# Zero fills of a gradient kernel: 56 KB rows for the last fills of the software queue

## The chip, the cores and the metric

The kernel runs on one core of one Trainium2 chip. The time is the device time of that core, in microseconds, for one launch. TensorE multiplies, VectorE and ScalarE do the elementwise work and empty PSUM, and 16 DMA engines move data between the device memory and the on-chip memory. Transfers are issued by SyncE and ScalarE (two hardware queues, q1 and q10 in the profile) and by GpSimd, which the profile calls POOL (one software queue, q0). [...]

## The reference

One decoding step of a network and the gradients of all its inputs: a layer norm, an attention that reads only the last W = 4096 rows of a cache of 32768, a gate from a small network with a squared ReLU, and a residual sum.

```python
W = min(4096, max(256, Sk // 4))
k = jnp.repeat(k_cache[:, :, Sk - W:, :], rep, axis=1)
v = jnp.repeat(v_cache[:, :, Sk - W:, :], rep, axis=1)
scores = jnp.einsum("bhqd,bhkd->bhqk", q, k) * (Dh ** -0.5)
p = _softmax(scores, axis=-1)
o = jnp.einsum("bhqk,bhkd->bhqd", p, v)
...
s = _A_ref(xn, A_k_cache, A_v_cache, A_wq, A_wo)
g = _silu(_B_ref(xn, B_w1, B_b1, B_w2, B_b2))
return x + s * g
...
_out, _vjp = jax.vjp(_f, A_x, A_k_cache, A_v_cache, A_wq, A_wo, B_w1, B_b1, B_w2, B_b2)
```

The sizes are: batch 2, one query position, model width 512, 32 query heads and 8 cache heads of 128, hidden width 1792 in the gate. All data is bf16. The outputs are the result and nine gradients. The gradients of the K cache and of the V cache (out_2 and out_3) have the shape of the caches, 2 x 8 x 32768 x 128 each. Only the last 4096 rows of each head are not zero: the other 28672 rows of each of the 32 pairs of batch and head are zeros that the kernel has to write.

## The kernel before

**Zero fills.** There are 32 fills of 28672 rows of 256 bytes, 7168 KB each, one per pair of cache and head; `zparts` (line 105) lists them. 31 are issued by GpSimd in the loop at lines 115 to 120, ahead of everything else on that engine, so they run in their order 0 to 30 on the software queue. Their source is one tile of zeros, `zt`, of 128 partitions and 112 x 128 bytes, and the transfer converts its uint8 to the type of the destination. The function `zf` (line 90) makes one transfer. A "row" here is one descriptor: a contiguous stretch of the output.

Most fills write two times 128 rows of 112 cache rows each, as bf16, so a descriptor is 28 KB. The fills listed in `zlong` (line 107) write 128 rows of 224 cache rows: there `zf` views the destination as 32-bit, so that the same 14336 elements of `zt` fill 56 KB. Five fills listed in `zshort` are cut into several transfers of other sizes. A fill is issued when the one eight transfers before it has landed. The last fill, number 31, is issued by SyncE at line 623, directly after the store of the gradient of w1 (line 618), and it waits for fill 29 of the software queue (line 624).

**Start.** SyncE loads w1, w2, wo, wq and the first V tile; the small network, the projections and the transposes of the weights follow (lines 216 to 347).

**Four rounds** (line 422), one for each batch and group of four cache heads. A round takes a V tile and a K tile of 4 MB (`nat`, 128 partitions of 32 KB) and computes scores, softmax and the gradients. `outer_store` (line 404) writes the gradient of the V tile over the tile itself and stores it from ScalarE's queue (line 414), then SyncE loads the next V tile into the same memory; the same for K. In round 3, the last one, there is no next load.

**Epilogue** (from line 498). The memory of the cache tiles is freed and given to the tiles of the epilogue, of which `o_rows` (line 502) is the first. ScalarE issues the store of the gradient of wq (line 500). Then come a chain of small steps, the store of the gradient of w2 (line 610), that of w1 (line 618), the last fill (line 623) and that of wo (line 630).

Of the kernel before, what the change touches and what calls it, by code (L numbers as in the profile page):

```python
# [16 lines left out]
def kernel(  # L17
# [86 lines left out]
    ZQ = 2 * B * HKV  # L104
    zparts = [(out_2, q) for q in range(B * HKV)] + [(out_3, q) for q in range(B * HKV)]

    zlong = (3, 5, 7, 11, 12, 16, 17, 18, 19, 22, 23, 24, 28)
    zshort = {
        2: ((5, 8, 2), (120, 68, 3), (128, 32, 1), (16, 1, 1)),
        4: ((3, 1, 2), (2, 99, 6), (128, 112, 1), (128, 102, 1), (86, 1, 1)),  # L110
# [547 lines left out]
```

## Time and profile before

| | |
|---|---|
| median of 6 runs | 775.14 us |
| the six runs | 766.73, 767.09, 767.11, 783.18, 799.6, 800.37 us |
| the profiled execution | 766.91 us |
| its span, first to last instruction | 765.1 us |
| busy share of TensorE / VectorE / ScalarE / GpSimd | 54% / 36% / 28% / 4% |
| bytes moved | 326.73 MB, mean 427 GB/s |
| q0, the fills from GpSimd | 227.55 MB, 70.4% of the 16 engines' time |
| q1, SyncE's transfers | 56.63 MB, 18.8% |
| q10, ScalarE's transfers | 41.95 MB, 12.9% |

The profile is that of one execution. "Busy" counts an engine's instructions, and a matmul's end is modelled. In the slices, a digit is the busy share of a fortieth of the span in tenths. In answers on DMA, a line gives a queue's packets, MB and the share of 16 engines' time; shares of a short window can go a little over 100%, since a packet counts whole by its start. In the chain and in the order of time, a line begins with the start and the length in us. `L414` is line 414 of the kernel.

### The profile page before, as it was taken

The page shows a single profiled execution, that of the slowest core. Times are in us where ns is not written, and L with a number is a line of the kernel's source. Part 1 is how long each engine was busy: PE and PEld are TensorE (multiplying, and loading weights), DVE is VectorE, ACT ScalarE, POOL GpSimd, SP SyncE. Part 2 cuts the span into 40 slices and gives each one's busy share as a digit, 9 for nine tenths or more (in the row PEclk, how much of TensorE's full clock was granted, in tenths as well). Part 3 has the DMA queues.
Part 4 walks back from the last instruction along what each step waited for, and adds up shares of the span by engine and source line. Part 5 has one row for each costly group of instructions (what it writes and reads, how often), then busy time and mean ns, then how long its engine had stood idle before and what let it go on. Part 6 is the DMA issues. An engine that isn't in the chain of part 4 may idle for free.

```text
span 765.1 us, 9402 instructions
## 1 busy us (share of the span) xinstructions
PE 414.8 (54%) x4118; PEld 271.7 (36%) x4118; DVE 277.2 (36%) x484; ACT 214.8 (28%) x313; POOL 30.3 (4%) x56
## 2 busy tenths in 40 slices
PE   0166776548800774891086847502654886176770
PEld 0153365435300673450045734102543543134220
DVE  3033343238510343842033455401323755024760
ACT  0034341044510123661011145500114355100350
POOL 3000010010000000000000000000000000000000
PEclk9997889686765796786558968755968677575555
DMA  9999999999999999999999999999999999999998
GB/s 353 432 427 428 438 423 431 437 430 429 421 436 428 433 436 435 424 428 433 428 430 438 439 430 422 430 433 433 439 436 428 420 433 429 441 422 428 427 429 364
DMA packets 12473, 326.73 MB, mean 427 GB/s; under 512 B 2276, under 2 KB 2284, under 8 KB 2294
## 3 DMA queue, kind: packets, MB, share of 16 engines
q0 software_dynamic: 8000, 227.55, 70.4%
q1 hardware_dynamic: 2696, 56.63, 18.8%
q10 hardware_dynamic: 1736, 41.95, 12.9%
q8 instruction: 32, 0.52, 0.3%
q14 instruction: 9, 0.07, 0.0%
HBM read 45.62 MB, written 280.50 MB: 426 GB/s over the span
## 4 chain that ended last, share of the span: by engine, by line
DMA 38%; PE 32%; DVE 15%; ACT 8%; issue 4%; ACTq 0%; DVEq 0%; SPq 0%
DMA out_dram<-nat 16%; DMA nat<-in_A_k_cache_dram 14%; PE ov L410 6%; PE s_ps L383 4%; DMA b_bf<-in_B_b_dram 4%; DMA nat<-in_A_v_cache_dram 4%; PE tp L377 4%; DVE tT L156 3%; DVE ds_bf L457 2%; ACT p_bf L444 2%; DVE nat L156 2%; PE wps L628 2%; ACT nat L154 2%; PE dops L308 1%; PE ps L399 1%
## 5 line engine op out<-in xcount | busy, mean ns | idle before, releaser
L377 PE MATMUL tp<-pperm,nat 128*128 128x128 bf16 x1024 | 85.7, 235 | 142.8 <-DMA nat<-in_A_v_cache_dram 111.2
L156 DVE COPY tT<-tp 128x1024 bf16<-128x1024 bf16 x96 | 64.1, 689 | 212.6 <-PE tp L377 212.0
L377 PEld LDWEIGHTS <-nat 128*128 128x128 bf16 x1024 | 74.9, 107 | 149.6 <-DMA nat<-in_A_v_cache_dram 113.1
L154 ACT COPY tT<-tp 128x1024 bf16<-128x1024 bf16 x32 | 32.4, 1012 | 273.8 <-PE tp L377 273.8
L154 ACT CAST nat<-ov 128x512 bf16<-128x512 f32 x160 | 87.6, 589 | 53.2 <-PE ov L410 52.0
L156 DVE CAST nat<-ov 128x512 bf16<-128x512 f32 x96 | 65.4, 690 | 49.2 <-PE ov L410 48.0
L410 PE MATMUL ov<-bd,ds_bf 128*128 128x512 bf16 x128 | 48.1, 454 | 5.8 <-DVE nat L156 3.9
L410 PE MATMUL ov<-bd,p_bf 128*128 128x512 bf16 x128 | 48.9, 451 | 4.3 <-DVE nat L156 1.8
L101 POOL DMA_DIRECT2D out_dram<-zt x47 | 28.7, 615 | 533.8 <-DMA out_dram<-zt 530.6
L383 PE MATMUL dp_ps<-tT,zdo 128*128 128x256 bf16 x256 | 42.2, 298 | 14.2 <-DVE tT L156 8.2
L383 PE MATMUL s_ps<-tT,zq 128*128 128x256 bf16 x256 | 40.0, 282 | 14.5 <-DVE tT L156 9.4
L383 PEld LDWEIGHTS <-zdo 128*128 128x128 bf16 x256 | 25.9, 105 | 22.9 <-issue 19.3
L399 PE MATMUL ps<-t,nat 128*128 128x16 bf16 x1024 | 28.5, 173 | 7.8 <-DVE bd L367 7.8
L383 PEld LDWEIGHTS <-zq 128*128 128x128 bf16 x256 | 24.9, 101 | 21.5 <-issue 19.0
L399 PEld LDWEIGHTS <-nat 128*128 128x128 bf16 x1024 | 28.5, 103 | 11.0 <-issue 5.8
L495 PE MATMUL wps<-dq_rows,xn_bf 2*128 2x512 bf16 x32 | 13.4, 485 | 24.3 <-ACT wq L154 19.0
L391 PE MATMUL tp<-ident_bf,p_bf 128*128 128x128 bf16 x64 | 7.5, 312 | 34.9 <-ACT p_bf L444 34.9
L444 ACT ACTIVATE p_bf<-e_sb,rl 32x512 bf16<-32x512 f32 x16 | 22.8, 1423 | 3.4 <-DVE rl L441 3.3
L156 DVE CAST wq<-wps 128x512 bf16<-128x512 f32 x16 | 11.0, 690 | 31.5 <-PE wps L495 31.1
L154 ACT CAST dw_st<-wps 128x512 bf16<-128x512 f32 x15 | 8.8, 587 | 47.9 <-PE wps L608 45.1
L457 DVE SCALAR_TENSOR_TENSOR ds_bf<-dp_ps,delta,p_bf 32x512 bf16<-32x512 f32 x16 | 21.7, 1357 | 0.3
L410 PEld LDWEIGHTS <-ds_bf 128*128 128x128 bf16 x128 | 13.0, 108 | 22.9 <-issue 19.7
(197 smaller groups left out, 458.6 us busy)
## 6 DMA issues: line engine op xcount, KB each, us to landing
out_dram<-zt POOLq DMA_DIRECT2D x26, 7168.0 KB, 162.0
out_dram<-nat ACTq DMA_DIRECT2D x8, 4096.0 KB, 28.4
nat<-in_A_v_cache_dram SPq DMA_DIRECT2D x4, 4096.0 KB, 30.5
nat<-in_A_k_cache_dram SPq DMA_DIRECT2D x4, 4096.0 KB, 30.3
out_dram<-zt POOLq DMA_DIRECT2D x4, 3584.0 KB, 56.2
out_dram<-zt SPq DMA_DIRECT2D x1, 7168.0 KB, 36.0
out_dram<-zt POOLq DMA_DIRECT2D x1, 6120.0 KB, 86.2
wo<-in_A_wo_dram SPq DMA_DIRECT2D x1, 4096.0 KB, 37.5
```

Of the source, the lines that this page charges most:

```text
L101: sw_fill.append(nc.gpsimd.dma_start(out=v, in_=zs))
L154: nc.scalar.copy(out=out_ap, in_=in_ap)
L156: nc.vector.tensor_copy(out=out_ap, in_=in_ap)
L308: nc.tensor.matmul(dops[0:B, :, :], lhsT=dsT_bf[:, dk, :], rhs=woT[:, :, dk, :], start=(dk == 0), stop=(dk == DK - 1))
L377: nc.tensor.transpose(tp[:, j, :], nat[:, g * CC + half * CH + j, :], pperm[:].rearrange("p b k -> p (b k)"))
L383: nc.tensor.matmul(out_ps[:, half * CH * PB:(half + 1) * CH * PB], lhsT=zbuf[:, pr, o:o + R], rhs=tT[:, :, pr, :], start=(g == 0 and pr == ...
L399: nc.tensor.matmul(ps[:], lhsT=nat[:, g * CC + half * CH + cc, :], rhs=cols[half][:, cc, :, g, :], start=(half == 0 and g == 0 and cc == 0 ...
L410: nc.tensor.matmul(ov[:], lhsT=src[:, cc].rearrange("r k b -> r (k b)"), rhs=bd[:, gh * 4:(gh + 1) * 4, :], start=True, stop=True)
L444: nc.scalar.activation(out=p_bf[rb, :, :, pr], in_=e_sb[rb], func=ACT.Copy, scale=rl[rb, 0:1])
L457: nc.vector.scalar_tensor_tensor(out=ds_bf[rb, :, :, pr], in0=dp_c[rb], scalar=delta[rb, 0:1], in1=p_bf[rb, :, :, pr], op0=ALU.subtract, o ...
L495: nc.tensor.matmul(wps[:], lhsT=xn_bf[:, k:D:DK], rhs=dq_rows[:, :], start=True, stop=True)
L628: nc.tensor.matmul(wps[:], lhsT=o_rows[:, j:N:NJ], rhs=ds_rows[:, :], start=True, stop=True)
```

## The change

Four numbers, 26, 27, 29 and 30, are added to `zlong`. Fill 28 is there already, so the last five fills of the software queue are all written as 128 descriptors of 56 KB. Fill 25 keeps its descriptors of 28 KB, and fill 31 on SyncE's queue is not touched.

```diff
-    zlong = (3, 5, 7, 11, 12, 16, 17, 18, 19, 22, 23, 24, 28)
+    zlong = (3, 5, 7, 11, 12, 16, 17, 18, 19, 22, 23, 24, 28, 26, 27, 29, 30)
```

The order of the fills, their bytes and all other instructions stay as they are.

## The prediction

> **What bounds the kernel now.** I read the slices of the page first. Below them stands the rate that the 16 DMA engines moved in each fortieth of the span.
>
> ```profile
> DMA  9999999999999999999999999999999999999998
> GB/s 353 432 427 428 438 423 431 437 430 429 421 436 428 433 436 435 424 428 433 428 430 438 439 430 422 430 433 433 439 436 428 420 433 429 441 422 428 427 429 364
> ```
>
> Between the first slice and the last the engines never idle and the rate stays near 430 GB/s. The kernel is as long as its 326.73 MB take. An edit that moves the same bytes can gain only by a better rate, and loses whatever time it leaves the engines without work. So I asked two things: does a 56 KB row move faster than two of 28 KB, and can the engines run dry? The row kinds, from DMA answers for windows of 10 us in which only the software queue (q0) moves data: 600 to 610 (28 KB rows), then 670 to 680 (56 KB rows).
>
> ```profile
> q0 software_dynamic: 148, 4.24, 100.2%
> ```
>
> ```profile
> q0 software_dynamic: 76, 4.36, 102.5%
> ```
>
> Columns are packets, MB and the share of 16 engines. A 28 KB row takes 1.002 x 160 engine-us / 148 = 1.083 us, a 56 KB row 1.025 x 160 / 76 = 2.158 us, twice 1.079. Per byte they are the same.
>
> Next, what the rows do to others. The same view for 648 to 658, where the last store of round 3 (q10, 32 KB rows) runs beside 28 KB fills, and for 541 to 550, where a cache load (q1, 32 KB rows) runs beside 56 KB fills:
>
> ```profile
> q10 hardware_dynamic: 66, 2.16, 50.8%
> q0 software_dynamic: 73, 2.09, 49.0%
> ```
>
> ```profile
> q0 software_dynamic: 47, 2.52, 65.2%
> q1 hardware_dynamic: 45, 1.47, 39.2%
> ```
>
> The two queues take turns row by row, whatever the row is long: 66 to 73, and 47 to 45. A 32 KB row takes 0.508 x 160 / 66 = 1.23 us. So a store loses speed when the fills beside it have longer rows.
>
> Which transfer matters is in the waits of ScalarE, in the chain that ended last (start, length), and in the DMA issues of ScalarE and SyncE in order of time:
>
> ```profile
> ACT o_rows L154 <- DMA out_dram<-nat: 20.4, 1, 20.4
> ```
>
> ```profile
> 638.66 25.43 DMA out_dram<-nat
> ...
> 664.19 1.00 ACT o_rows L154
> ```
>
> ```profile
> 617.24 0.56 ACTq L414 DMA_DIRECT2D out_dram<-nat  x1
> 638.66 0.55 ACTq L414 DMA_DIRECT2D out_dram<-nat  x1
> 672.12 0.37 ACTq L500 DMA_DIRECT2D out_dram<-wq  x1
> 742.59 0.35 ACTq L630 DMA_DIRECT2D out_dram<-wo  x1
> ```
>
> ```profile
> 720.82 0.33 SPq L610 DMA_DIRECT2D out_dram<-dw_st  x1
> 727.80 0.33 SPq L618 DMA_DIRECT2D out_dram<-dw_st  x1
> 728.18 0.43 SPq L623 DMA_DIRECT2D out_dram<-zt  x1
> ```
>
> The epilogue's first tile, o_rows, lies in the memory of the cache tiles, so it waits for the K store of round 3, from 638.66 to 664.09. From there a chain of small steps leads to the dw1 store (727.80), the last fill behind it on SyncE (728.18) and the wo store (742.59). Meanwhile the software queue has work until about 730.8. The cover is thin: the late transfers are issued 3 us before it is used up.
>
> **What the Trainium skill says.** "DMA: Bandwidth & Descriptors", section "Queues, rings and completion order", says that each engine goes round the queues that have work at packet granularity, draining a packet before it switches, and that a packet typically holds 9 to 17 descriptors. The first half agrees (47 turns to 45); here a turn is one row of up to 56 KB. The same page, "Issuing engines are not separate DMA queues", says that transfers from all engines interleave on the same 16; the windows above show that. Its "Specifications" give a ceiling of 435 GB/s; the page's 420 to 441 between the first slice and the last say that longer rows have nothing to win.
>
> **The change part by part.** Fill 28 has 56 KB rows already, so four fills change: 26, 27, 29 and 30. Each issues 128 rows where it issued 256, the same 7.34 MB, in the same order. Counting 256 rows per short fill back from the switches in the row sizes (594, 664, 685), fill 26 is served from about 612, 27 until 664, 28 from there to 685, 29 and 30 until 731. Up to 612 nothing changes: POOL issues a fill when the fill eight before it has landed, and the last issue is at 563.48, before any changed row is served.
>
> *Rows saved*: 512 rows fewer, each pair at most 2 x 1.083 - 2.158 = 0.008 us cheaper. 512 x 0.008 / 16 = 0.26 us, within the reading error. I take zero (bounds 0 and -0.3). Fewer rows to generate costs POOL nothing: it idles 126.7 us before its next instruction.
>
> *V store, issued 617.24*. Its issue does not move, since no load is outstanding after 557. Its first rows appear at 623.7: queue 10 moves nothing from 617.3 to 623.5. That is 6.5 us, the time of rows already queued ahead. The wq store shows the same with 56 KB rows ahead: issued 672.12, no row before 682.5, its first ones by 682.7, so 10.6 us. The V store then starts at 617.24 + 10.6 = 627.8. It has 128 rows, 8 for each engine, and each waits for a turn of the fills: 8 x (1.23 + 2.16) = 27.1 us, done at 654.9. Before it was 8 x (1.23 + 1.08) = 18.5, and 623.7 to 641.8 was measured.
>
> *K store, issued 638.66*. It now queues behind the V store and follows with no gap: another 27.1 us, done at 682.0. Before, its last row ended at 662.7 and the landing was seen at 664.1, so I add 1.4: 683.4. The delay is X = 683.4 - 664.1 = 19.3 us. Bounds: if the V store still starts at 623.7 and each takes 26 us (what a load from 531.5 to 557.5 took, mostly beside 56 KB rows), X = 623.7 + 52 + 1.4 - 664.1 = 13. If the fills get 148 rows to 128 (the count over that load), a store takes (128 x 1.23 + 148 x 2.16) / 16 = 29.8 and X = 627.8 + 59.6 + 1.4 - 664.1 = 24.7. I take the even turns.
>
> *What queues behind*. ScalarE stops at o_rows; behind it are its copies of wq, so TensorE waits too (19.0 us now), then the whole chain from 664 on. I move it as a block by X: wq store at 691.4, dw2 store 740.1, dw1 store 747.1, last fill 747.5, wo store 761.9. The block could shrink or grow by some 2 us with TensorE's granted clock (0.50 to 0.66 there).
>
> *What covers it*. While the stores are slow the fills are fast, so the cover is used up sooner. From 612 the fills have 36.7 MB. Alone until 627.8 at 430 GB/s: 6.8. In 16 turns on 16 engines: 16 x 16 x 57344 B = 14.7. Alone again from 682.0 until the wq store's first row at 691.4 + 10.6 = 702.0: 8.6. The last 6.6 MB are 7.2 rows per engine beside wq rows: 7.2 x 3.39 = 24.4, until 726.4, and the rest of wq until 727.4. Then nothing is issued until 740.1. The engines stand idle for some 13 us and again for about 3 us between the dw2 store's data (4.3 us) and the dw1 store.
>
> *The end*. Dw1, last fill and wo are 1.84 + 7.34 + 4.19 = 13.37 MB. From 731 to the end of the span just such an amount was moved, 13.47 MB in 34.1 us with its ragged tail, so 33.8 us. Dw1 is issued at 747.1; a first row comes 1.0 us after issue on idle engines (SyncE's first load: issued 0.74, moving at 1.74) up to 3.4 (the wo store, 742.59 to 746.0, behind other rows); I take 1.3. The end is at 747.1 + 1.3 + 33.8 = 782.2. The wo store (761.9 + its 18.6 to landing = 780.5) fits inside. The span grows from 765.1 to 782.2, by 17.1. In general the growth is X - 2.2, so the delay is free up to 2.2 us.
>
> The profiled execution took 766.91 us, 1.8 around its span; with 17.1 it is 784.0. The six runs shown have three at 766.7 to 767.1, like the profiled one, and three at 783 to 800; their median of 775.14 is 8.2 above the profiled one. A median of such a mix after would be up to 8 above 784.
>
> **The rivals.**
> *Hidden*: turns are shared by bytes, or o_rows waits for something else that ends at the same time. Then X is under 2.2 and the time is 766.9. For it: the chain infers its releasers. Against: 45 turns to 47 beside 56 KB rows, where equal bytes would give 60 to 34, and a wait of 20.4 us that ends with the landing. Chance 0.06.
>
> *Faster*: longer rows move better and the stores are not hurt. The place is 612 to 731. The page's slices vary from 422 to 441 there; if 29.4 MB went at 441 instead of 430, 1.7 us are won and the time is 765.2. It decides only if X stays below 2.2 + 1.7 = 3.9. Against: 1.079 beside 1.083 us for the same bytes. Chance 0.03.
>
> *Worse*: the fills get more than their turn (X = 24.7): 766.9 + 22.5 = 789.4. *Milder*: X = 13 gives 777.7. Both are the forecast's mechanism with other sizes, and lie in its chance of 0.91. That the change does nothing is excluded: fills with 56 KB rows are already served as one row each (76 rows, 4.36 MB).
>
> **How the numbers follow.** Forecast 784.0, slower, 0.91; hidden 0.06; faster 0.03. Under 0.2% (1.5 us) a measurement of this kernel could not tell a change from none. The range goes from 777.7 less 2 for the epilogue's clock, 775.5, to 789.4 plus 8 for a mixed median, 797.5; the 0.09 of the rivals stay outside.
>
> **What would show it.** Until 612 nothing differs. The K store's time to landing goes from 25.4 to about 45 us, ScalarE's wait for o_rows from 20.4 to about 40. The rate per slice dips well under 400 near 727 to 742, where it was 430. The wq store takes some 25 us for its data. The dw1 store and last fill are issued near 747, the wo store near 762. The forecast is wrong if the K store lands before 667, or if the dry stretch is missing though it lands late, for instance because the software queue still holds rows at 740.

## The result and the profile after

The changed kernel takes 791.45 us in the median of 10 runs (782.93 to 817.4), the kernel before in the same comparisons 782.5 us in the median of 20 (766.56 to 801.92). Five of the 10 executions and 11 of the 20 took 15 to 35 us longer than the shortest of their kernel, and the ratio leaves those out. It is 1.0221, with a 95% interval of 1.0209 to 1.0234: slower by 2.2%. The five shortest executions of the changed kernel took 782.93 to 784.41 us.

The profiled execution took 798.27 us, 796.5 of it span. That is 14 to 15 us longer than the five shortest, about as long as one late landing that is shown below. (The landing of a transfer is the moment when its completion is seen.) First the slices of its page:

```profile
DMA  9999999999999999999999999999999999994089
GB/s 362 430 432 425 431 433 438 419 442 417 430 435 429 436 438 415 431 434 429 434 438 436 427 422 434 430 429 442 438 417 447 423 430 435 434 426 196 1 369 395
```

The rate is as before until the last four slices. Then it falls to 196 and 1 GB/s: the engines have nothing to do, where the same two slices of before have 428 and 427. The transfers that ran beside the last fills, in the DMA answer for 660 to 670 (packets, MB, share of 16 engines):

```profile
q0 software_dynamic: 49, 2.75, 63.9%
q10 hardware_dynamic: 48, 1.57, 37.6%
```

Turns are even (49 to 48), and the store gets 157 GB/s where it had 216 beside 28 KB rows. ScalarE's wait and its DMA issues, then SyncE's last ones:

```profile
ACT o_rows L154 <- DMA out_dram<-nat: 47.2, 1, 47.2
```

```profile
617.61 0.55 ACTq L414 DMA_DIRECT2D out_dram<-nat  x1
646.59 0.56 ACTq L414 DMA_DIRECT2D out_dram<-nat  x1
707.09 0.37 ACTq L500 DMA_DIRECT2D out_dram<-wq  x1
777.67 0.35 ACTq L630 DMA_DIRECT2D out_dram<-wo  x1
```

```profile
755.88 0.33 SPq L610 DMA_DIRECT2D out_dram<-dw_st  x1
762.87 0.33 SPq L618 DMA_DIRECT2D out_dram<-dw_st  x1
763.25 0.43 SPq L623 DMA_DIRECT2D out_dram<-zt  x1
```

The V store is issued within 0.4 us of where it was before, so up to there nothing was lost here. The wait for o_rows grows from 20.4 to 47.2 us, and everything behind it moves. Between 729 and 755 the DMA answer has next to nothing:

```profile
DMA packets 149, 0.02 MB, mean 1 GB/s; under 512 B 146, under 2 KB 148, under 8 KB 148
```

The part of the delay that is peculiar to this execution is seen in 683.6 to 698.9, when the store's rows are through and its queue has one packet left:

```profile
q0 software_dynamic: 121, 6.54, 100.4%
q10 hardware_dynamic: 1, 0.00, 6.1%
```

That one small packet took 0.061 x 16 x 15.3 = 14.9 us, and o_rows starts at 699.07. The numbers for a landing in time come from the experiments.

### The profile page after: what moved, and what is told of

Its sections match the earlier page's. It is cut to its first block, busy times and chain, and to the rows that moved or that the text cites. A ratio compares the mean times of both kernels' runs of the same rounds, so it can differ in the third digit from the quotient of the medians.

```text
span 796.5 us, 9402 instructions
## 1 busy us (share of the span) xinstructions
PE 412.6 (52%) x4118; PEld 268.2 (34%) x4118; DVE 277.4 (35%) x484; ACT 214.7 (27%) x313; POOL 29.5 (4%) x56
## 4 chain that ended last, share of the span: by engine, by line
PE 32%; DMA 32%; DVE 14%; ACT 8%; another core or an unknown queue 6%; issue 5%; ACTq 0%; DVEq 0%; SPq 0%
DMA out_dram<-nat 11%; DMA nat<-in_A_k_cache_dram 9%; DMA nat<-in_A_v_cache_dram 8%; PE ov L410 5%; PE tp L377 4%; PE s_ps L383 4%; DMA b_bf<-in_B_b_dram 4%; DVE tT L156 3%; PE dp_ps L383 3%; DVE ds_bf L457 2%; ACT p_bf L444 2%; DVE nat L156 2%; PE wps L628 2%; ACT tT L154 2%
## 5 line engine op out<-in xcount | busy, mean ns | idle before, releaser
L383 PE MATMUL dp_ps<-tT,zdo 128*128 128x256 bf16 x256 | 41.8, 296 | 15.1 <-DVE tT L156 8.6
L383 PEld LDWEIGHTS <-zq 128*128 128x128 bf16 x256 | 24.7, 100 | 21.0 <-issue 18.6
L483 PEld LDWEIGHTS <-wqT 128*128 128x128 bf16 x128 | 4.5, 101 | 52.2 <-issue 51.0
## 6 DMA issues: line engine op xcount, KB each, us to landing
wo<-in_A_wo_dram SPq DMA_DIRECT2D x1, 4096.0 KB, 37.3
```

Of the source, the lines that this page charges most:

```text
L383: nc.tensor.matmul(out_ps[:, half * CH * PB:(half + 1) * CH * PB], lhsT=zbuf[:, pr, o:o + R], rhs=tT[:, :, pr, :], start=(g == 0 and pr == ...
```

## The experiments

Theory A is the forecast's: the longer rows slow the V and K stores of round 3, the epilogue comes late, and the DMA engines run dry. Its rivals are named in the expectations.

**The changed kernel once more (again, again2).** No edit.

> The changed kernel once more, for a second look at where the time goes. Theory A (the late store): the K store of round 3 lands near 683 us, o_rows waits about 40 us for it, the engines are dry for some 15 us before the dw2 store, and the span is near 782, ratio 1.022. Rival B (the rows themselves cost more): the span grows by the same, but the fills are served later already from 612 us on, and no dry stretch is seen.

> The changed kernel again, for one look at an execution whose landings come in time. Theory A (the late store): the K store lands within 2 us of 683, the dw1 store is issued near 747, the wo store near 762, the span is 781 to 783.

Ratio of again 1.021 (1.0186 to 1.0235). Both profiles fell on executions with a late landing (spans 815.4 and 799.6): the last K load took 54.1 and 49.5 us to land, where it took 37.3 before, and the V store is issued only at 654.30 and 628.77. That load had landed before the first changed row was served (612), so the delay is not the change's, and these profiles don't test the numbers of the K store. The next run does.

**Fills 26 and 27 alone (only_26_27), and 29 and 30 alone (only_29_30).**

```diff
-    zlong = (3, 5, 7, 11, 12, 16, 17, 18, 19, 22, 23, 24, 28)
+    zlong = (3, 5, 7, 11, 12, 16, 17, 18, 19, 22, 23, 24, 28, 26, 27)   # only_26_27
+    zlong = (3, 5, 7, 11, 12, 16, 17, 18, 19, 22, 23, 24, 28, 29, 30)   # only_29_30
```

> 56 KB rows for fills 26 and 27 alone, the two that are served beside the V and K stores of round 3. Theory A: all of the loss, ratio 1.022, since fill 28 has such rows already and the K store is done before fill 29 begins. Rival B (a cost of each longer row, wherever it is served): half of the loss, ratio 1.011. Rival C (the loss comes from fills 29 and 30, which slow the wq store and empty the queue): ratio 1.000.

> 56 KB rows for fills 29 and 30 alone, served from 685 us on, beside the wq store. Theory A: ratio 1.000 within 0.002, the wq store takes some 27 us for its data instead of 19 and nothing waits for it. Rival B: ratio 1.011. Rival C: ratio 1.022.

With 26 and 27 the ratio is 1.0226 (1.0165 to 1.0286), the whole loss within its interval, at a span of 780.4. With 29 and 30 the profiled execution took 766.68 us, at a span of 764.9, and the second short one 767.18. The other two of four took 816.91 and 817.5, about 50 us more and longer than any execution of the kernel before. They were not profiled, so what these rows do in a long execution is open, and there is no ratio. The chain of waits of both, start and length of the K store's wait:

```profile
645.81 38.91 DMA out_dram<-nat
```

```profile
635.61 25.02 DMA out_dram<-nat
```

And the wq store of only_29_30 beside 56 KB rows, in 690 to 700:

```profile
q0 software_dynamic: 48, 2.75, 64.0%
q10 hardware_dynamic: 47, 1.54, 37.2%
```

The wq store is slowed just as the others are (47 to 48 turns), and in the short executions it costs nothing, since nothing waits for it. For these, rivals B and C fall: the same rows cost 2.2% beside the V and K stores and nothing beside the wq store.

**V tile in front (swap_after).** The change, with the V tile first in the pool of the cache tiles:

```diff
+    vfirst = kvp.tile([P, NCB * DH], BF16, tag="v")
     w12 = kvp.tile([P, NCB * DH], BF16, tag="k")
...
-        nat = kvp.tile([P, NCB * DH], BF16, tag=tag)
+        nat = vfirst if (tag, r) == ("v", 0) else kvp.tile([P, NCB * DH], BF16, tag=tag)
```

> The changed kernel's fills, but the V tile lies in front of the K tile in the pool, so that the first tiles of the epilogue take the memory of the V tile and wait for the V store, which is issued 21 us before the K store. Theory A: o_rows waits until about 660 instead of 683, earlier than in the kernel before (664), so the loss is gone: ratio 0.998 to 1.002, and no dry stretch. Rival B: the rows are as long as in the changed kernel, so the loss stays: ratio 1.022. Rival C: the loss stays too.

Ratio 1.0223 (1.0203 to 1.0244): the loss stays, against theory A's expectation. The chain shows what happened:

```profile
644.58 40.52 DMA out_dram<-nat
...
685.20 1.00 ACT o_rows L154
```

o_rows still waits for the K store, although the V tile lies in front. Perhaps its instruction waits for both stores, whatever memory it takes; the profile names only the wait that ended last. The edit did not take the wait away, so it tells nothing about rivals. It is of use as one more execution with the changed fills whose K store lands in time (685.10). Giving the epilogue memory of its own was not tried. That o_rows' wait is the gate is therefore shown by doses (only_26_27, only_29_30, short_26_27), not by its removal. From the start of o_rows to the dw1 store it is 63.5 us here, 63.6 in the kernel before, and 61.9 to 64.0 in all profiles: the block moves nearly whole.

**The change in the other direction (short_26_27).** Rows of 14 KB:

```diff
         10: ((4, 69, 2), (128, 112, 1), (128, 107, 1), (88, 1, 1)),
+        26: ((128, 56, 4),),
+        27: ((128, 56, 4),),
```

> The kernel before with rows of 14 KB for fills 26 and 27, the change in the other direction. A turn beside a store row then takes 1.23 + 0.54 = 1.77 us. Theory A: the V store starts near 621 and takes 14 us, the K store starts near 643, takes 14 us and lands near 658 instead of 664; ScalarE waits 14 to 16 us for o_rows instead of 20.4. The epilogue's stores are issued 4 to 6 us earlier, and the span stays, since the engines never run dry and the bytes set it: ratio 0.998 to 1.001. Rival B (each row costs by its length or number, wherever it is served): ratio away from 1 by 0.005 or more.

Ratio 1.0002 (0.9982 to 1.0021); three of its six executions took 781.9 to 783.48. The turns stay even with this third length of row, and the store now gets 290 GB/s (622 to 635):

```profile
q10 hardware_dynamic: 115, 3.77, 68.7%
q0 software_dynamic: 112, 1.61, 29.5%
```

The chain:

```profile
636.34 21.41 DMA out_dram<-nat
657.86 1.00 ACT o_rows L156
```

The K store lands at 657.75 (658 expected), the dw1 store is issued at 719.76 instead of 727.80 (2 us of that are a V store issued at 615.17), and the span is 764.9. An earlier epilogue wins nothing in the short executions, because the bytes set the end: the cost has one side only.

**One fill alone (only_26, only_27).**

```diff
-    zlong = (3, 5, 7, 11, 12, 16, 17, 18, 19, 22, 23, 24, 28)
+    zlong = (3, 5, 7, 11, 12, 16, 17, 18, 19, 22, 23, 24, 28, 26)   # only_26
+    zlong = (3, 5, 7, 11, 12, 16, 17, 18, 19, 22, 23, 24, 28, 27)   # only_27
```

> 56 KB rows for fill 26 alone. Theory A: fill 26 is served from 612 until about 629, and what it does is to hold back the V store's first row from 623.7 to about 628.8. After that the rows beside both stores have 28 KB: V until 647, K until 666, landing at 667, X = 3, of which 2.2 are free. Ratio 1.000 to 1.003. Rival B (each longer row costs the same wherever it is served): a quarter of the loss of the four, ratio 1.0055.

> 56 KB rows for fill 27 alone, served beside the end of the V store and the K store; fill 28 behind it has them already. Theory A: the V store starts at 623.7 as in the kernel before and ends near 644, the K store then takes 27 us, from 644 or, if its own first row is held back, from 649: landing at 673 to 678, X = 9 to 14, ratio 1.009 to 1.015. Rival B: ratio 1.0055.

The ratio of only_26 is 1.0198 (1.017 to 1.0226), where theory A expected 1.000 to 1.003 and rival B 1.0055; its four executions took 780.07 to 783.42. The four of only_27 took 783.14 to 801.24, three of them near 801, and there is no ratio. Neither answers its question. In only_26 the V store is issued at 626.90 instead of 617.24, because the last K load took 48.2 us to its landing (37.3 before):

```profile
nat<-in_A_k_cache_dram SPq DMA_DIRECT2D x1, 4096.0 KB, 48.2
```

That landing, at 574.6, precedes the first changed row (612). In only_27 the same load took 53.7 us, and the V store is issued at 650.50. So a delay that has nothing to do with fills 26 or 27 is in both profiled executions; the six others were not profiled, and the share of each fill stays open. It also pointed to late landings as a thing to study by itself.

**More work for the engines (cover_after, cover_before).** Fill 31 goes to the software queue behind fill 30; lines 619 to 625 fall away.

```diff
-    for qi in range(ZQ - 1):
+    for qi in range(ZQ):
...
-    with tc.issue_after(last.ins):
-        fin = nc.sync.dma_start(out=v, in_=zs)
```

> The changed kernel with fill 31 on the software queue, behind fill 30, with rows of 28 KB, instead of on SyncE behind the dw1 store. The epilogue is as late as in the changed kernel, but the engines have 7.34 MB more to move meanwhile. Theory A (the loss is time without work for the engines): no dry stretch of more than 3 us before the dw1 store; the wo store, issued near 762, is the last thing, 10 us of rows and about 3 for issue and landing: span 774 to 777, ratio 1.012 to 1.015. Rival D (the chain of the late epilogue sets the end by itself): span 781 to 783, ratio 1.021.

> The kernel before with fill 31 on the software queue behind fill 30, instead of on SyncE behind the dw1 store. Theory A: nothing is lost or won where landings come in time, ratio 0.999 to 1.002. Where a landing is held and the epilogue comes 16 us late, the fill covers part of it: the wo store, then issued near 759, ends the span near 773, so 774 to 776 in place of 783. Rival E (the long executions of the kernel have nothing to do with late landings at the end): they stay at 783 and 800.

cover_after has ratio 1.0133 (1.011 to 1.0156), span 774.4. Its wo store is issued at 762.36 and lands 11.1 us later. In 727 to 739, where only_26_27 with the same late epilogue is dry (0.02 MB in 728 to 739), it has:

```profile
q0 software_dynamic: 178, 5.10, 100.3%
```

This is as theory A expected: the epilogue is as late as with the change (o_rows at 684.97), but the engines move 7.34 MB meanwhile, and the span of 782.3 (swap_after) becomes 774.4. Rival D falls. What is left has a cause of the same kind: the data of the dw1 store end near 753, the wo store is issued only at 762.36, and in between the engines are dry again. In 751 to 763 there is only:

```profile
q1 hardware_dynamic: 68, 0.75, 14.7%
```

In cover_before the executions took 768.71, 776.85 and four times 793.26 to 794.94, the kernel before beside them 766.63 to 766.79, 783.25 to 784.57 and 800.2 to 801.15. The long ones shrink by 7 us, as expected, and the short one grows by 2, which was not (ratio 1.0079, 0.9989 to 1.0169). The profiled execution is that of 776.85: its last K load took 50.1 us to land and its V store is issued at 630.37. Up to there it has the rows of the kernel before, so the late landing does not need the change. A long execution of the kernel before itself was never profiled.

**No rows of 56 KB at all (rows28), and this with fill 31 moved (cover_rows28).**

```diff
-    zlong = (3, 5, 7, 11, 12, 16, 17, 18, 19, 22, 23, 24, 28)
+    zlong = ()
```

> No fill has rows of 56 KB: the thirteen long ones have 28 KB too. Theory F (a landing is held until fill rows that are already queued on the same engine are through, so shorter rows hold it half as long): the K load of round 3, which lands beside fill 22 or 23, lands 2 to 4 us after its last row instead of 5.5, the V store of round 3 is issued 2 to 5 us before 617, ratio 0.998 to 1.001, and no execution takes more than 777. Rival E: the rows change nothing in the spread, executions near 783 and 800 as before.

> Both together: fill 31 on the software queue, and no rows of 56 KB. Theories A and F: the epilogue is early and covered, so that all executions stay within 1.5 us of 767, ratio 0.998 to 1.001, where the kernel before has executions at 783 and 800. Rival E: executions near 783 and 800 remain.

rows28: ratio 1.0007 (0.9992 to 1.0022), and all six executions within 767.18 to 767.37, where 7 of 11 of the kernel before took 783 to 801. The last K load lands in 25.4 us instead of 37.3, and the whole epilogue is earlier (DMA issues of SyncE, then the chain):

```profile
699.14 0.33 SPq L610 DMA_DIRECT2D out_dram<-dw_st  x1
706.13 0.33 SPq L618 DMA_DIRECT2D out_dram<-dw_st  x1
715.97 0.39 SPq L623 DMA_DIRECT2D out_dram<-zt  x1
```

```profile
619.15 24.95 DMA out_dram<-nat
644.20 1.00 ACT o_rows L154
```

The dw1 store comes 22 us earlier than before. The V store of round 3 is issued at 597.88, 19 us earlier and not 2 to 5. Of these, 5.5 us are there when the last K load is issued (520.22 for 525.68), so the long rows of earlier rounds have a share, and 11.9 come from that load. The bytes set the end, so the best time is the same, but there is now room for a late landing. cover_rows28 took 769.01 to 769.37 (1.0032, 1.0017 to 1.0047): no spread either, and 2 us longer than rows28, which was not expected. Its end is a fill on the software queue instead of SyncE's; the reason for the 2 us stays open. cover_before has them too, so they may be in cover_after as well.

**The change where there is slack (rows28_last5).** 56 KB rows for fills 26 to 30 and no other.

```diff
-    zlong = (3, 5, 7, 11, 12, 16, 17, 18, 19, 22, 23, 24, 28)
+    zlong = (26, 27, 28, 29, 30)
```

> 56 KB rows for the last five fills, 26 to 30, and for no other: the change on a kernel whose epilogue comes some 20 us earlier (the dw1 store at 706 instead of 728). Theory A: the K store is slowed as in the changed kernel and lands 10 to 19 us later than without the long rows (there 639 to 642), but this delay is smaller than the time until the fills run out, near 731, so nothing is lost: ratio 0.999 to 1.003. Rival B (the long rows of these fills cost time by themselves): ratio 1.02 as in the changed kernel.

Ratio 1.0004 (0.9995 to 1.0013); 13 of 14 executions took 766.76 to 767.1, one 783.71. The chain:

```profile
614.36 37.13 DMA out_dram<-nat
651.59 1.00 ACT o_rows L154
```

The K store takes 37.1 us to land instead of 24.95, and o_rows starts 7 us later than in rows28 (the V store ran ahead of the long rows). The dw1 store, at 714.37, still comes before the fills run out, and nothing is lost. The rows of the last five fills thus cost only what the missing slack makes of them. The test is milder than planned, with a delay of 7 us and not 10 to 19.

**Which long rows make landings late (without_22_24, with_22_24).**

```diff
-    zlong = (3, 5, 7, 11, 12, 16, 17, 18, 19, 22, 23, 24, 28)
+    zlong = (3, 5, 7, 11, 12, 16, 17, 18, 19, 28)   # without_22_24
+    zlong = (22, 23, 24)                            # with_22_24
```

> The kernel before with 28 KB rows for fills 22, 23 and 24, which are served from about 535 to 595, beside the last K load. Theory F (rows of 56 KB hold the landing of that load, and what is lost there comes out at the end): the last K load takes 25 to 28 us to its landing instead of 37, the V store of round 3 is issued before 610, and all executions stay near 767. Rival G (the long rows of the earlier rounds, fills 3 to 19, are the cause): executions near 783 and 800 remain.

> 56 KB rows for fills 22, 23 and 24 and for no other. Theory F: the last K load takes 36 to 49 us to its landing, and executions near 783 come back beside ones near 767. Rival G: all executions near 767.

without_22_24: ratio 1.0002 (0.9993 to 1.0011), 13 of 14 executions below 767.2 and one at 784.63. with_22_24: 1.0004 (0.9995 to 1.0012), all 13 within 766.82 to 767.29. In the same comparison 12 of 35 of the kernel before took 782 to 802. The last K load lands in 25.8 us in without_22_24, as theory F has it, but the V store is issued at 613.83 and not before 610. In with_22_24 it lands in 27.1, where 36 to 49 were expected, and the executions near 783 did not come back:

```profile
nat<-in_A_k_cache_dram SPq DMA_DIRECT2D x1, 4096.0 KB, 27.1
```

It is issued there at 516.79 instead of 525.68, so it is nearly over when fill 22 comes. Long rows for fills 22 to 24 are thus not enough by themselves; without them one long execution in 14 was left. Earlier long rows make the rounds late, and the later a load is, the more it meets long rows; this reading fits the profiles but was only argued.

## Why the forecast was right and where it was wrong

**Even turns, row by row: right.** Beside 56 KB rows the windows of 10 us have 48 or 49 rows of the fills to 47 or 48 of a store (after, only_26_27, only_29_30), and beside 14 KB rows it is 112 to 115 in 13 us. The Trainium skill's round of queues at packet granularity ("DMA: Bandwidth & Descriptors", "Queues, rings and completion order") agrees with this: the profile counts each row as one packet. How many descriptors such a packet holds, it does not show.

**The stores: right to 2 us.** In the profile after, the DMA answer for 617.7 to 629.5 has the software queue alone: the V store's rows are held back for 12 us (10.6 forecast). The K store landed at 684.7 in only_26_27 and at 685.1 in swap_after, forecast 683.4.

**"K store, issued 638.66": wrong, without effect.** It was issued at 644.58 to 646.59 (swap_after, only_26_27, after). TensorE stands still for 5.56 us in the chain of only_26_27:

```profile
630.16 5.56 issue
```

No releaser is shown. The store waits behind the V store's rows until about 655 anyway.

**The block moved by X, the dry stretch, the end: right, the sum in part by luck.** In swap_after the dw2 store is issued at 741.73, dw1 at 748.71, wo at 763.51 (740.1, 747.1 and 761.9 forecast), and the span is 782.3 (782.2). The line of the dw1 store:

```profile
748.71 0.33 SPq L619 DMA_DIRECT2D out_dram<-dw_st  x1
```

From there to the end of the span it is 33.6 us, and it is 33.6 or 33.7 in the profiles of after, again, again2, only_26_27, only_26 and only_27 too: once the engines are dry, the end follows the dw1 store. The forecast had 35.1. Before it was 37.3, so the dw1 store could be issued up to 731.5 for nothing, which is 3.7 us later, and not 2.2. Against that X was 21.0 in swap_after (685.1 less 664.1) instead of 19.3. The two errors cancel, so that 17.2 us of span came out where 17.1 were forecast. In only_26_27 the block took 1.6 us less, and X is 20.6 for a growth of 15.3. In the ratio of short executions, too, 784.0 / 766.91 = 1.0223 agrees with the measured 1.0221 more closely than its terms do.

Single slices pass the 435 GB/s that the prediction took as a ceiling (441 before, 447 after). That longer rows win nothing rests on the 1.083 and 2.158 us.

**The number for the median: wrong.** This step failed. The 784.0 is 766.91 plus 17.1: it counts from a profiled execution of the short kind, and what the long executions add to a median stands in it at nothing. "A median of such a mix after would be up to 8 above 784" went only into the range. But the median of the kernel before is one of a mix as well, 775.14 in the six runs shown and 782.5 in the twenty. Beside these, 784.0 says a growth of 8.9 or 1.5 us, where the sum has 17.1 and the short executions grew by 2.2%. The measured median was 791.45, 7.5 above 784.0.

The term that stood at nothing has this size: 5 of 10 executions of the changed kernel and 11 of 20 of the kernel before are 15 to 35 us longer. The prediction read the last K load as over at 557; that is about its last row, and it landed at 563.0. In five profiled executions (again, again2, only_26, only_27, cover_before) this load took 48 to 54 us to land instead of 37.3, and the V store was issued at 627 to 654 instead of 617. So "its issue does not move" holds for some executions and not for others. With a dry end each such delay is passed on: o_rows starts 16.8 and 34.3 us later in again2 and again than in swap_after, and the span is 17.3 and 33.1 longer.

The experiments show on what the long group depends. Without rows of 56 KB there were no long executions (0 of 12, in two kernels); with the 13 fills of such rows there were between 2 of 7 and 7 of 11 in a comparison. Why a landing comes late in one execution and not in the next stays open.

**The rivals.** "Hidden" and "faster" needed X below 2.2 or 3.9; it was 21. "Worse" (24.7) and "milder" (13) were both further from it than the 19.3 of the forecast.

## What to carry to other kernels

Where queues take turns row by row, as here, the length of a bulk transfer's rows acts as a priority: a store of round 3 got 290, 216 and 157 GB/s beside rows of 14, 28 and 56 KB. Give short rows to background fills that run beside a transfer somebody waits for, and long ones only where nothing waits. In a kernel bound by bytes, ask what work is left when the last dependent chain delivers its stores; in these runs a delay was free up to that point and cost in full beyond it. Where runs of a kernel fall into groups, look at what makes the long ones and not only at the best case: rows28 stays within about 0.1% of the best time of the kernel before, in all six of its runs, at a median of 767.25 us beside 784.34.

## What the runs showed that was not expected

The last small packet of a store, the one after its rows, took 14.9 us in the profile after, as long as about seven rows of 56 KB (7 x 2.16 = 15.1). The Trainium skill says in "DMA: Bandwidth & Descriptors", "Queues, rings and completion order", that the semaphore's increment is written only after every earlier write of that DMA engine, across its queues. The measured length fits that, with long rows of another queue as the earlier writes; no run isolated it.
